# Moving single steps of a written-out order: chunk attention with an FFN on one core

## The chip, the core and the metric

The kernel runs on one core of a Trainium2 chip. A core has engines that run side by side, each with an instruction line of its own that it works off in order: TensorE for matmuls (PE; its loading of weights is PEld), VectorE (DVE), ScalarE (ACT), GpSimd (POOL) and SyncE (SP), which here issues all the DMAs. The metric is the device time of one execution in microseconds (us); smaller is better.

## The reference

Attention in chunks of 64 rows, and on its output, laid side by side for the 8 heads, a feed-forward layer, all in fp32:

```python
batch, n_heads, seq, head_dim = (8, 8, 576, 64)          # chunk = 64
scores = scale * np.matmul(q_c, k_c.transpose(0, 1, 2, 4, 3))   # per chunk: 64 x 64
scores = scores - np.max(scores, axis=-1, keepdims=True)
attn = np.exp(scores)
attn = attn / (np.sum(attn, axis=-1, keepdims=True) + 1e-09)
out = np.matmul(attn, v_c)
x = np.ascontiguousarray(attn_out.transpose(0, 2, 1, 3)).reshape(B * S, H * D)   # 4608 x 512
h = x @ w_in                                              # 512 x 2048
g = h * (1.0 / (1.0 + np.exp(-1.702 * h)))
return (g @ w_out).astype(np.float32)                     # 2048 x 512
```

## The kernel before

**The work.** Every large product is done in fp32 precision with three matmuls, since each operand is split in a high and a low part (x_h, x_l; g_h, g_l): low times high, high times high, high times low. The 4608 rows of x are 36 tiles of 128. Attention runs over pairs of tiles, named by the first tile u of the pair (tq0_16 is a step of the pair 16, 17). For one pair, function plan_pair loads q and k into one buffer "raw" (lines 953, 964), turns them with two big transposes on DVE, tq0 and tq1 (1007), makes scores s on PE (1023), their maximum mx and the difference m on DVE (1031, 1040), exp on ACT (1043), the sum z on DVE (1047 to 1050), the normalisation on POOL (1053), transposes et on DVE (1072), and x on PE (1097). "raw" comes free when tq1 has read it, and only then may the next pair's loads start.

**The FFN** runs over 9 blocks of 512 rows (4 tiles) and 16 slices of 128 columns of w_in; g numbers slices through all blocks, so that 0 to 15 are block 0 and 32 is the first of block 2. For a slice: h0_g and h_g on PE (1245), gelu and its high part gh_g on ACT, the low part gl_g on DVE (1272), then o_g_0 to o_g_3 on PE (1282 to 1284), one for each tile, which add to four sums po0 to po3. After a block's last slice a sum is copied out by ob_n_t (n the block, t the tile): by ACT for t even (1291), by DVE for t odd (1293), into one of two buffers "ob"; the store st_n_t (1298) is issued on SP, and its landing frees the buffer. The sum of the next block can't start before the copy is done.

**Blocks 0 and 1** are computed so. Block 2 (plan_seven) and the pairs of blocks 3 to 8 (plan_two, numbered 0 to 2 by r) get x @ w_in from seven products of half-size pieces instead of eight. In block 2 the products' matmuls are ph0_g to ph3_g (715 to 717), their drains on DVE d0_g to d3_g (719), the low part of gelu gl_g (756). The pieces of w_in are sums and differences made on DVE (612, steps plo and pout with their high parts on ACT) and POOL (592 to 601), stored to DRAM (628) and loaded again (702, ld0_g to ld3_g; 801). The pieces of x come from subtractions (535, steps t1 to t4 with x_r_h behind; plan_x), whose engine the table ON_POOL sets: POOL for r = 0, DVE for the rest.

**The order** is written out before the program is built. The class Plan takes every step with an engine, a cost in us, a rank, the events that it needs and makes, and the buffers that it takes and gives; `emit` plays it through and, whenever an engine is free, gives it the ready step of the lowest rank. A DMA's landing is reckoned from constants (ISSUE, LANDING, LANES). The engines' lines are then fixed in the order so found, and at run time each engine waits at the head of its line, whatever stands behind. The first steps up to about 60 us come from a list of names, ORDER.

Of the kernel before, what the change touches and what calls it, by code (L numbers as in the profile page):

```python
# [47 lines left out]
class Plan:  # L48
# [7 lines left out]

    ISSUE, LANES, LANDING = 0.48, 8, 2.1
    TABLE_LOAD = 1.3

    def __init__(self, buffers):  # L60
        self.free = dict(buffers)
        self.steps = []
        self.landed = [0.0] * self.LANES
        self.first = {}


    def add(self, engine, cost, rank, fn, need=(), make=None, take=(), give=(), table=None, port=False):
        self.steps.append((engine, cost, rank, fn, tuple(need), make, tuple(take), tuple(give), table, port or engine == POOL))
# [4 lines left out]
    def transfers(self, now, count, each):  # L73

        for _ in range(count):
            start = max(now, self.landed[-self.LANES])
            now = start + self.ISSUE
            self.landed.append(max(start + self.LANDING, self.landed[-1] + each))
        return now, self.landed[-1]

    def emit(self):
        waits, users, ready = {}, {}, {e: [] for e in self.HANDOVER}
        at = []
# [16 lines left out]
        while left:  # L100
            for e, heap in ready.items():
                while heap and busy[e] <= now + 1e-9:
# [11 lines left out]
                    if pick is None:  # L114
                        break
                    _, cost, _, fn, _, make, take, give, tab, port = self.steps[pick]
                    if first.get(e):
# [15 lines left out]
                    busy[e] = now + cost  # L133
                    post(done, 0, give)
                    if e != DMA:
# [26 lines left out]
def tile_chunk_attention_ffn(  # L162
# [14 lines left out]
    P = 128  # L177
# [4 lines left out]
    TB = 4  # L182
# [66 lines left out]
    def plan_w(j):  # L249
# [98 lines left out]
    def plan_first(u):  # L348
# [171 lines left out]
    def plan_x(r, h, ua, uc, rank):  # L520
# [266 lines left out]
    def plan_two(s, p):  # L787
# [137 lines left out]
    def plan_pair(u):  # L925
# [198 lines left out]
        if pe:  # L1124
            for t in range(2):
                plan.add(
                    DMA, (2, 0.85), rank - 3, lambda t=t: load_qk_rows(t), need=[ev("rows0")] if t else [],
                    make=ev(f"rows{t}"), take=[] if t else [raw_tag],
# [13 lines left out]
        else:  # L1142
# [83 lines left out]
    def plan_ffn(g):  # L1226
# [104 lines left out]
        for t in range(TB):  # L1331
# [83 lines left out]
```

## Time and profile before

| | |
|---|---|
| median of 3 runs | 845.12 us (843.11 to 847.92) |
| the profiled execution | 844.18 us |
| its span, first to last instruction | 842.4 us, so 1.8 us lie around it |
| mean granted TensorE clock | 0.993 of full |
| busy: PE, PEld, DVE, ACT, POOL | 818.4, 680.0, 549.1, 378.4, 86.7 us |
| DMA | 128.96 MB, mean 153 GB/s |

The rows in the prediction are read so. A row of busy time by stretch gives the stretch and its length, then for PE, PEld, DVE, ACT and POOL the busy time and (x) the number of instructions, then the granted clock of TensorE, the busy share of the DMA engines and the GB/s. A row of waits says who waited for whom: total, times, longest. A row of a timeline has the start, the duration, the engine and the line of the kernel, the operation and its operands (out<-in, buffer numbers left out), the shape, and in brackets how long the engine had been idle before it and what ended that. SPq is SP's line of DMA issues: their duration is that of the issuing, not of the transfer. 512-wide matmuls start 0.23 us apart when nothing holds them, though each is shown with 0.39.

### The profile page before, as it was taken

What the parts mean: (1) busy time and instruction counts of PE and PEld (TensorE: products, weight loads), DVE (VectorE), ACT (ScalarE), POOL (GpSimd) and SP (SyncE); (2) the same over time, 40 slices, a digit from 0 to 9 for tenths busy, and PEclk for the clock granted to TensorE, in tenths of its full rate; (3) what the DMA queues carried; (4) which work ended last, traced back from release to release, by engine and by line L of the source; (5) the groups of instructions that cost most, each with busy time, mean ns of one, the idle gap of its engine ahead of it and who ended that gap; (6) DMA issues with size and microseconds to landing.
All of it is one profiled execution on the core that took longest, in us unless ns stands there. A gap on an engine that the chain in (4) does not pass through costs nothing.

```text
span 842.4 us, 15212 instructions
## 1 busy us (share of the span) xinstructions
PE 818.4 (97%) x5894; PEld 680.0 (81%) x5894; DVE 549.1 (65%) x781; ACT 378.4 (45%) x557; POOL 86.7 (10%) x78
## 2 busy tenths in 40 slices
PE   7999998999979999999999999999999999999998
PEld 6878886877878888778888888888888888888786
DVE  5769967566867888874776995393778453443422
ACT  5989825345344436342534433342555323223322
POOL 1000163563200000000000100000001000000000
PEclk9999999999989999999999999999999999999999
DMA  9997856775488776575466336466541054444101
GB/s 227 313 309 239 251 130 163 208 202 134 129 244 218 212 209 141 169 175 147 125 179 176 62 79 173 126 152 155 145 128 49 1 165 121 118 122 126 50 1 51
DMA packets 238248, 128.96 MB, mean 153 GB/s; under 512 B 186464, under 2 KB 208992, under 8 KB 238176
## 3 DMA queue, kind: packets, MB, share of 16 engines
q1 hardware_dynamic: 238176, 127.98, 56.5%
q8 instruction: 47, 0.77, 0.4%
q14 instruction: 25, 0.20, 0.1%
HBM read 103.81 MB, written 24.12 MB: 152 GB/s over the span
## 4 chain that ended last, share of the span: by engine, by line
PE 81%; SPq 9%; DMA 4%; DVE 3%; issue 1%; ACT 1%; POOL 0%; DVEq 0%; ACTq 0%; POOLq 0%
PE po L1282 14%; PE po L1283 13%; PE po L1284 13%; PE hp L810 9%; PE hp L811 9%; PE hp L812 9%; SPq L964 3%; SPq L338 2%; PE hp L1245 2%; PE hp L1246 2%; PE hp L1247 2%; DMA w<-seven 2%; PE s L1023 2%; PE x L1097 1%; SPq L258 1%
## 5 line engine op out<-in xcount | busy, mean ns | idle before, releaser
L1282 PE MATMUL po<-w,g_l 128*128 128x512 f32 x576 | 228.1, 396 | 6.7 <-ACT ob L1291 4.8
L1283 PE MATMUL po<-w,g_h 128*128 128x512 f32 x576 | 225.0, 391 | 0.0
L1284 PE MATMUL po<-w,g_h 128*128 128x512 f32 x576 | 224.8, 390 | 0.0
L1282 PEld LDWEIGHTS po<-w,g_l 128*128 128x128 f32 x576 | 108.5, 188 | 32.3 <-ACT ob L1291 5.5
L1284 PEld LDWEIGHTS po<-w,g_h 128*128 128x128 f32 x576 | 108.4, 188 | 23.0
L1283 PEld LDWEIGHTS po<-w,g_h 128*128 128x128 f32 x576 | 108.5, 188 | 21.1
L848 ACT ACTIVATE g<-g 128x512 f32<-128x512 f32 x48 | 30.3, 632 | 143.3 <-DVE g L795 143.1
L1072 DVE STREAM_TRANSPOSE eT<-e 32x512 f32<-32x512 f32 x120 | 84.2, 701 | 5.4 <-POOL e L1053 3.5
L810 PE MATMUL hp<-w,w 128*128 128x512 f32 x224 | 87.4, 390 | 0.2
L811 PE MATMUL hp<-w,w 128*128 128x512 f32 x224 | 87.2, 389 | 0.0
L812 PE MATMUL hp<-w,w 128*128 128x512 f32 x224 | 87.2, 389 | 0.0
L1053 POOL TENSOR_TENSOR e<-e,r 128x1024 f32<-128x1024 f32 x16 | 32.2, 2012 | 502.1 <-DVE r L1050 397.6
L857 DVE TENSOR_TENSOR g_l<-g,g_h 128x512 fp32r<-128x512 f32 x48 | 35.2, 737 | 44.5 <-ACT g_h L853 44.2
L853 ACT ACTIVATE g_h<-g 128x512 fp32r<-128x512 f32 x48 | 30.3, 631 | 73.7 <-PE po L1284 71.4
L1007 DVE STREAM_TRANSPOSE qkT<-raw 128x1024 f32<-128x1024 f32 x30 | 37.2, 1241 | 27.8 <-DMA raw<-in_k_dram 15.7
L1245 PE MATMUL hp<-x_l,w 128*128 128x512 f32 x120 | 47.8, 398 | 5.8 <-DVE g_l L1272 5.8
L810 PEld LDWEIGHTS hp<-w,w 128*128 128x128 f32 x224 | 42.0, 188 | 9.9 <-DVE f L795 0.5
L812 PEld LDWEIGHTS hp<-w,w 128*128 128x128 f32 x224 | 42.0, 188 | 8.8
L811 PEld LDWEIGHTS hp<-w,w 128*128 128x128 f32 x224 | 42.0, 188 | 8.6
L1247 PE MATMUL hp<-x_h,w 128*128 128x512 f32 x120 | 47.4, 395 | 0.0
L1246 PE MATMUL hp<-x_h,w 128*128 128x512 f32 x120 | 47.4, 395 | 0.0
L795 DVE TENSOR_TENSOR d<-hp,d 128x512 f32<-128x512 f32 x48 | 32.9, 684 | 19.0 <-PE hp L812 18.7
(142 smaller groups left out, 1335.5 us busy)
## 6 DMA issues: line engine op xcount, KB each, us to landing
w<-seven SPq DMA_DIRECT2D x120, 256.0 KB, 2.9
pieces<-seven SPq DMA_DIRECT2D x56, 256.0 KB, 2.9
seven<-w SPq DMA_DIRECT2D x24, 512.0 KB, 3.7
w<-seven SPq DMA_DIRECT2D x24, 512.0 KB, 4.6
raw<-in_moe_w_in_dram SPq DMA_DIRECT2D x16, 512.0 KB, 7.5
raw<-in_moe_w_out_dram SPq DMA_DIRECT2D x16, 512.0 KB, 7.8
out_dram<-ob SPq DMA_DIRECT2D x32, 256.0 KB, 2.3
raw<-in_q_dram SPq DMA_DIRECT2D x208, 32.0 KB, 2.4
```

The source lines that it names most:

```text
L810: nc.tensor.matmul(hp, w[:, 0, c], xl[:, c], start=c == 0, stop=False)
L811: nc.tensor.matmul(hp, w[:, 0, c], xh[:, c], start=False, stop=False)
L812: nc.tensor.matmul(hp, w[:, 1, c], xh[:, c], start=False, stop=c == 1)
L857: nc.vector.tensor_tensor(gl, words(h, late), gh.bitcast(F32), op=ALU.subtract)
L1007: nc.vector.transpose(st["tr"][:, i].rearrange("p n (t j) -> p (n t) j", j=32), st["raw"][:, i].rearrange("p n t j -> p (n t) j"),)
L1072: nc.vector.transpose(st["et"][po : po + 32, :, 32 * a : 32 * a + 32], st["e"][pi : pi + 32, :, 32 * b : 32 * b + 32],)
L1245: nc.tensor.matmul(hp, wh, xl, start=cc == 0, stop=False)
L1246: nc.tensor.matmul(hp, wh, xh, start=False, stop=False)
L1247: nc.tensor.matmul(hp, wl, xh, start=False, stop=cc == NCC - 1)
L1282: nc.tensor.matmul(po, gl[:, c], w[:, 0, :], start=first, stop=False)
L1283: nc.tensor.matmul(po, gh[:, c], w[:, 0, :], start=False, stop=False)
L1284: nc.tensor.matmul(po, gh[:, c], w[:, 1, :], start=False, stop=last)
```

## The change

The constants and ranks of the planner change, and a table NUDGE adds an offset to the rank of 38 single steps. The model of a DMA gets a limit on pieces in flight (PIECES); LANDING goes from 2.1 to 1.8; the 16 pairs get other RANKS; stores get a rank 40 ahead of their slice instead of 22 (STORE); the high and low parts of late slices get 7.5 instead of 1.5 (GLATE); the pieces of weights are made a step nearer or further (LEAD, SUMS); and POOL does the subtractions of r = 2 as well (ON_POOL), eight instructions. Nothing else is computed otherwise: all other instructions are the same, with the same shapes, on the same engines. ORDER isn't changed.

```diff
-    ISSUE, LANES, LANDING = 0.48, 8, 2.1
+    ISSUE, LANES, LANDING = 0.48, 8, 1.8
+    PIECES = 3072
...
+        rank += self.nudge.get(make, 0.0)
...
             start = max(now, self.landed[-self.LANES])
+            while True:
+                flight = [(t, n) for t, n in self.flight if t > start]
+                if sum(n for _, n in flight) + pieces <= self.PIECES:
+                    break
+                start = flight[0][0]
             now = start + self.ISSUE
-            self.landed.append(max(start + self.LANDING, self.landed[-1] + each))
+            self.landed.append(max(start + self.LANDING, self.landed[-1]) + each)
...
-    RANKS = (-10.5, 9.0, 14.0, 21.0, 26.5, 28.5, 35.0, 39.0, 45.5, 49.5, 61.0, 72.0, 76.5, 85.5, 94.0, 101.5)
+    RANKS = (-14.0, 8.5, 15.5, 21.0, 26.5, 30.5, 34.5, 39.5, 45.5, 54.5, 59.5, 76.5, 77.0, 78.5, 94.0, 101.5)
...
-    LEAD = 27
+    LEAD = 28
...
-    SUMS = 3
-    ON_POOL = (0,)
+    SUMS = 2
+    GLATE = 7.5
+    XLATE = 0.5
+    STORE = 40
...
+    NUDGE = {
+        "ph0_36": -2.0, "o_15_1": 2.0, "ph2_40": -12.5, "o_12_2": 6.5, "o_63_1": -1.5, "o_36_3": 1, "d0_0_3":
...
+    ON_POOL = (0, 2)
...
-            at = o_rank(g) - 1.5 if late else rank - 5
+            at = o_rank(g) - GLATE if late else rank - 5
...
-                    DMA, (len(list(spans((n * TB + t) * P, P))), 0.72), rank - 22, lambda t=t: o_store(t), need=[f"ob_{n}_{t}"],
+                    DMA, (len(list(spans((n * TB + t) * P, P))), 0.72), rank - STORE, lambda t=t: o_store(t), need=[f"ob_{n}_{t}"],
```

Lines of the kernel after the change are 25 to 27 further down (1298 is 1324, 1007 is 1033, 1272 is 1298, 756 is 782). What the change does to the lines of the engines is shown at three places. A row has the line, the operation, out<-in with the buffers' full names, the shape, and a count where alike instructions follow one another.

DVE in the second half of block 0, before and after. g_l_14 is the output of gl_14, the two transposes of raw_8 are tq0_8 and tq1_8, the copies ob_0_1 and ob_0_3 drain block 0:

```order
L1007 STREAM_TRANSPOSE qkT_8_1303<-raw_8_1069 128x1024
L1272 TENSOR_TENSOR g_l_14_1295<-hp_14_1226,g_h_14_1294 128x512
L1007 STREAM_TRANSPOSE qkT_8_1303<-raw_8_1069 128x1024
L1272 TENSOR_TENSOR g_l_15_1348<-hp_15_1287,g_h_15_1347 128x512
L1031 TENSOR_REDUCE m_8_1437<-s_8_1361 128x16
```

```order
L314 TENSOR_TENSOR w_15_1220<-wtmp_15_1164,w_15_1220 128x2x512
L1033 STREAM_TRANSPOSE qkT_8_1291<-raw_8_1067 128x1024 x2
L1298 TENSOR_TENSOR g_l_14_1305<-hp_14_1232,g_h_14_1304 128x512
L1298 TENSOR_TENSOR g_l_15_1337<-hp_15_1296,g_h_15_1336 128x512
L1057 TENSOR_REDUCE m_8_1438<-s_8_1358 128x16
```

Both transposes now stand ahead of gl_14. A little later in the same line z_8 goes behind gl_17 and two of the weight sums of line 612.

SP at the end of block 1, before and after. raw_16 is loaded in four lots of eight and more, w_7 and so on are weights' pieces, out_0_dram<-ob_1_t is st_1_t:

```order
L702 DMA w_7_754<-seven_80 128x1024
L953 DMA raw_16_2182<-in_k_dram 32x4x32 x8
L702 DMA w_8_821<-seven_80 128x512
L702 DMA w_0_331<-seven_80 128x1024
L953 DMA raw_16_2182<-in_k_dram 32x4x32 x8
L1298 DMA out_0_dram<-ob_1_0_2461 128x512
L1298 DMA out_0_dram<-ob_1_1_2474 128x512
L338 DMA v_14_2573<-in_v_dram 128x8x64
L702 DMA w_1_446<-seven_80 128x1024
L953 DMA raw_16_2182<-in_k_dram 32x4x32 x8
L702 DMA w_5_650<-seven_80 128x1024
```

```order
L728 DMA w_7_754<-seven_80 128x1024
L979 DMA raw_16_2180<-in_k_dram 32x4x32 x8
L1324 DMA out_0_dram<-ob_1_0_2441 128x512
L728 DMA w_8_821<-seven_80 128x512
L1324 DMA out_0_dram<-ob_1_1_2511 128x512
L979 DMA raw_16_2180<-in_k_dram 32x4x32 x8
L1324 DMA out_0_dram<-ob_1_2_2551 128x512
L728 DMA w_0_328<-seven_80 128x1024
L728 DMA w_1_440<-seven_80 128x1024
L979 DMA raw_16_2180<-in_k_dram 32x4x32 x8
L1324 DMA out_0_dram<-ob_1_3_2596 128x512
L728 DMA w_5_644<-seven_80 128x1024
```

The first two stores go ahead of a lot of eight loads, the third ahead of the last lot, and the weights w_0 and w_1 go behind.

DVE at the same place, before and after. g_l_32 is gl_32, d_32 and f_32 are what the drains d0 to d3 write, w_10 and w_12 are steps l0x and l1x on pieces of x, raw_16 is read by tq0_16 and tq1_16:

```order
L1293 COPY ob_1_1_2474<-po_1_1_1548 128x512
L756 TENSOR_TENSOR g_l_32_2477<-d_32_2395,g_h_32_2476 128x512
L1007 STREAM_TRANSPOSE qkT_16_2551<-raw_16_2182 128x1024
L1031 TENSOR_REDUCE m_14_2562<-s_14_2480 128x16
L719 TENSOR_TENSOR f_32_2453<-hp_32_3_2564,d_32_2395 128x256
L1040 TENSOR_TENSOR e_14_2561<-s_14_2480,m_14_2562 128x1024
L1293 COPY ob_1_3_2608<-po_1_3_1560 128x512
L756 TENSOR_TENSOR g_l_33_2605<-f_32_2453,g_h_33_2604 128x512
```

```order
L1319 COPY ob_1_3_2596<-po_1_3_1562 128x512
L576 TENSOR_TENSOR w_10_963<-xs_12_2529,w_9_881 128x2x256
L782 TENSOR_TENSOR g_l_32_2585<-d_32_2395,g_h_32_2584 128x512
L576 TENSOR_TENSOR w_12_1023<-xs_12_2529,w_11_1017 128x2x256
L782 TENSOR_TENSOR g_l_33_2600<-f_32_2563,g_h_33_2599 128x512
L745 TENSOR_TENSOR d_34_2618<-hp_34_0_2570,d_34_2618 128x256
L745 TENSOR_TENSOR d_34_2618<-hp_34_1_2603,d_34_2618 128x256 x2
L1073 TENSOR_REDUCE z_14_2642<-e_14_2535 128x16
L1074 TENSOR_SCALAR z_14_2642<-z_14_2642 128x16
L1076 RECIPROCAL r_14_2645<-z_14_2642 128x16
L1033 STREAM_TRANSPOSE qkT_16_2519<-raw_16_2180 128x1024
L745 TENSOR_TENSOR d_34_2618<-hp_34_2_2647,d_34_2618 128x256
```

gl_32 stood right behind ob_1_1 and stands now behind ob_1_3; tq1_16 stands ahead of the last drains of slice 34 (d2_34, d3_34), which it followed before. On ACT ob_1_2 goes ahead of gh_32, with the first two high parts of x's pieces behind it, and on PE o_32_0 and o_32_1 go behind ph1_34.

More of the change, by code (lines that the diff above doesn't have):

```diff
@@ L63, in __init__, with add, transfers @@
         self.landed = [0.0] * self.LANES
+        self.flight = []
         self.first = {}
-    def add(self, engine, cost, rank, fn, need=(), make=None, take=(), give=(), table=None, port=False):
-        self.steps.append((engine, cost, rank, fn, tuple(need), make, tuple(take), tuple(give), table, port or engine == POOL))
+        self.nudge = {}
+    def add(self, engine, cost, rank, fn, need=(), make=None, take=(), give=(), table=None, port=False, after=0.0):
+        rank += self.nudge.get(make, 0.0)
+        self.steps.append((engine, cost, rank, fn, tuple(need), make, tuple(take), tuple(give), table, port or (engine == POOL and not after), after))
     def bulk(self, cost, rank, fn, need=(), make=None, take=(), give=()):
         self.add(DMA, (1, cost), rank, fn, need=need, make=make, take=take, give=give)
-    def transfers(self, now, count, each):
+    def transfers(self, now, count, each, pieces=256):
         for _ in range(count):
             start = max(now, self.landed[-self.LANES])
+            while True:
[3 more added lines that the diff above has]
+                start = flight[0][0]
             now = start + self.ISSUE
-            self.landed.append(max(start + self.LANDING, self.landed[-1] + each))
+            self.landed.append(max(start + self.LANDING, self.landed[-1]) + each)
+            self.flight = flight + [(self.landed[-1], pieces)]
         return now, self.landed[-1]
@@ L115, in emit @@
                         break
-                    _, cost, _, fn, _, make, take, give, tab, port = self.steps[pick]
+                    _, cost, _, fn, _, make, take, give, tab, port, after = self.steps[pick]
                     if first.get(e):
@@ L133, in emit @@
                     busy[e] = now + cost
-                    post(done, 0, give)
+                    post(done + after, 0, give)
                     if e != DMA:
@@ L191, in tile_chunk_attention_ffn @@
     NH = 2
-    RANKS = (-10.5, 9.0, 14.0, 21.0, 26.5, 28.5, 35.0, 39.0, 45.5, 49.5, 61.0, 72.0, 76.5, 85.5, 94.0, 101.5)
+    RANKS = (-14.0, 8.5, 15.5, 21.0, 26.5, 30.5, 34.5, 39.5, 45.5, 54.5, 59.5, 76.5, 77.0, 78.5, 94.0, 101.5)
     K_ACT = (1, 2, 3, 4)
-    LEAD = 27
+    LEAD = 28
     PREP = -3
-    SUMS = 3
-    ON_POOL = (0,)
+    SUMS = 2
+    GLATE = 7.5
+    XLATE = 0.5
+    STORE = 40
+    OBODD = 0.0
+    RLATE = 0
+    NUDGE = {
[6 rows of a table added]
+    }
+    ON_POOL = (0, 2)
     RING_2 = (7, 8, 0, 1, 5, 6)
@@ L297, in plan_w @@
         e = lambda n: f"{n}_{j}"
-        plan.add(DMA, (2, 1.56), rank - 5.5, load, need=need, make=e("raw"), take=[f"w{j}"])
+        plan.add(DMA, (2, 1.5, 384), rank - 5.5, load, need=need, make=e("raw"), take=[f"w{j}"])
         plan.add(ACT, 1.08, rank, scale, need=[e("raw")], make=e("wsc"))
@@ L457, in plan_first @@
         rank = u - 95
-        plan.add(DMA, (1, 1.2), u - 103, lambda: load(0), make=ev("q"), take=[slot(0)])
-        plan.add(DMA, (1, 1.2), u - 102.9, lambda: load(1), make=ev("k"))
-        plan.add(DMA, (1, 0.9), u - 101.5, load_v, make=ev("v"), take=[slot(1)])
+        plan.add(DMA, (1, 1.2, 1024), u - 103, lambda: load(0), make=ev("q"), take=[slot(0)])
+        plan.add(DMA, (1, 1.2, 1024), u - 102.9, lambda: load(1), make=ev("k"))
+        plan.add(DMA, (1, 0.9, 1024), u - 101.5, load_v, make=ev("v"), take=[slot(1)])
         plan.add(PE, 0.45, rank, lambda: t_pe(0), need=[ev("q")], make=ev("tqp"), take=["hp"])
@@ L551, in lo @@
             nc.vector.tensor_tensor(conv(i, k, 1), form(raw(i, k)), conv(i, k, 0).bitcast(F32), op=ALU.subtract)
+        rank += XLATE
         e = lambda a: f"{a}x_{r}_{h}"
@@ L1126, in plan_pair @@
                 plan.add(
-                    DMA, (2, 0.85), rank - 3, lambda t=t: load_qk_rows(t), need=[ev("rows0")] if t else [],
+                    DMA, (2, 0.85, 1024), rank - 3, lambda t=t: load_qk_rows(t), need=[ev("rows0")] if t else [],
                     make=ev(f"rows{t}"), take=[] if t else [raw_tag],
@@ L1148, in plan_pair @@
                     plan.add(
-                        DMA, (count, 0.18), rank - ahead, lambda i=i, n=n: load_qk(i, n),
+                        DMA, (count, 0.18), rank - ahead - RLATE, lambda i=i, n=n: load_qk(i, n),
                         need=raw[:1] if i + n else [f"qk_1_{NP - 1}_{u - 2}"] if u - 2 >= NPE else [], make=ev(f"qk_{i}_{n}"),
@@ L1159, in plan_pair @@
             plan.add(
-                DMA, (2, 0.85) if pe else (len(list(spans(u * P, P))), 0.9), rank - (7 if pe else 1.5), lambda t=t: load_v(t), need=[ev("v0")] if t else [], make=ev(f"v{t}"),
+                DMA, (2, 0.85, 512) if pe else (len(list(spans(u * P, P))), 0.9, 1024), rank - (7 if pe else 1.5), lambda t=t: load_v(t), need=[ev("v0")] if t else [], make=ev(f"v{t}"),
                 take=[] if t else ["v"],
@@ L1341, in plan_ffn @@
                 plan.add(
-                    eng, 0.6, rank - 3.5, lambda t=t: o_out(t), need=[f"o_{g}_{t}"],
+                    eng, 0.6, rank - 3.5 + OBODD * (t % 2), lambda t=t: o_out(t), need=[f"o_{g}_{t}"],
                     make=f"ob_{n}_{t}", take=[tag], give=[f"po{t}"],
@@ L1367, in tile_chunk_attention_ffn @@
         plan.first[e] = names
+    plan.nudge.update(NUDGE)
     for u in range(TB):
```

5 rows, old and new, of the table NUDGE are left out of this document.

## The prediction

> **What bounds the kernel now.** I read the page first, then busy time by stretch, then the waits of TensorE (PE), then the timelines of the four other queues round its longest waits.
>
> ```profile
> span 842.4 us, 15212 instructions
> PE 818.4 (97%) x5894; PEld 680.0 (81%) x5894; DVE 549.1 (65%) x781; ACT 378.4 (45%) x557; POOL 86.7 (10%) x78
> ```
>
> PE is busy 97% of the span, so only 842.4 - 818.4 = 24.0 us are idle, plus what a lowered clock costs. The columns of the next view are PE, PEld, DVE, ACT, POOL busy, the granted PE clock, the DMA share, GB/s.
>
> ```profile
> 126.00:147.00 21.00, 17.66 (x72) 14.08 (x71) 14.59 (x20) 10.53 (x15) 7.32 (x7) 0.92 0.64 164
> 147.00:210.00 63.00, 60.55 (x502) 49.52 (x501) 38.48 (x47) 28.80 (x43) 29.63 (x30) 1.00 0.67 183
> 210.00:253.00 43.00, 38.17 (x326) 33.73 (x325) 32.45 (x49) 17.89 (x28) 7.45 (x6) 0.92 0.65 185
> 253.00:320.00 67.00, 65.23 (x742) 57.63 (x742) 56.06 (x95) 28.77 (x45) 3.81 (x2) 1.00 0.77 204
> 320.00:400.00 80.00, 79.46 (x470) 65.03 (x469) 59.05 (x88) 33.83 (x51) 3.81 (x2) 1.00 0.64 162
> 400.00:800.00 400.00, 399.60 (x2524) 329.08 (x2523) 243.32 (x351) 155.13 (x241) 11.94 (x6) 1.00 0.45 119
> ```
>
> From 400 to 800 PE idles 0.40 us: nothing can be won there, only lost. What can be won lies from 126 to 400: idle 3.34, 2.45, 4.83, 1.77 and 0.54. Two stretches also run at 0.92 of the clock, which costs 0.08 x 21 = 1.7 and 0.08 x 43 = 3.4. The whole prize is 12.9 + 5.1 = 18.0, or 2.1%. The start and the tail, the rest of the idle time, keep their order.
>
> ```profile
> PE hp L1245 <- DVE g_l L1272: 5.8, 3, 3.3
> PE po L1282 <- ACT ob L1291: 4.8, 1, 4.8
> ```
>
> Two waits hold 3.3 and 4.8 of it. Their releasers are copies that had waited themselves, so I follow each back.
>
> **Block 0's stores.** PE, SP and DVE, first the matmul h0_18:
>
> ```profile
> 129.72 0.39 PE L1247 MATMUL hp<-x_h,w 128*128 128x512 f32 x1
> 133.45 0.50 PE L1245 MATMUL hp<-x_l,w 128*128 128x512 f32 x1 [3.34 <-DVE g_l L1272]
> 134.92 0.63 PE L1247 MATMUL hp<-x_h,w 128*128 128x512 f32 x1
> 128.67 0.87 SPq L1298 DMA_DIRECT2D out_dram<-ob  x2
> 130.97 0.69 DVE L1293 COPY ob<-po 128x512 f32<-128x512 f32 x1 [6.15 <-DMA out_dram<-ob]
> 132.72 0.68 DVE L1272 TENSOR_TENSOR g_l<-hp,g_h 128x512 fp32r<-128x512 f32 x1
> 116.81 0.39 PE L1282 MATMUL po<-w,g_l 128*128 128x512 f32 x1
> 117.52 1.25 DVE L1007 STREAM_TRANSPOSE qkT<-raw 128x1024 f32<-128x1024 f32 x1 [3.31 <-DMA raw<-in_k_dram]
> ```
>
> The drain at 130.97 waited for the landing of a store that SP issued at 128.67, and g_l stood behind it in DVE's line. After the wait matmuls take 0.63 instead of 0.39. In the new order these stores keep their place on SP (st_0_3 alone goes behind a v load, 0.45), so the release at 133.45 stays. But tq1_8, the transpose of 117.52, now stands ahead of gl_14. It ends at 118.77, gl_14 at about 119.4, and o_14_0, which ran at 116.81, waits 2.6 for it. That wait comes out of the 3.34: the idle time is split in 2.6 and 0.7 and costs nothing new. What it may end is the lowered clock. The 1.56 below was followed by 0.39 to 0.40; 3.34 by 0.63.
>
> ```profile
> 202.45 0.50 PE L1245 MATMUL hp<-x_l,w 128*128 128x512 f32 x1 [1.56 <-DVE g_l L1272]
> 202.79 0.40 PE L1246 MATMUL hp<-x_h,w 128*128 128x512 f32 x1
> ```
>
> 2.6 lies between them. I take no lowered clock: **-1.7** (0 to -1.7).
>
> **Block 1's stores.** SP, DVE, ACT, PE:
>
> ```profile
> 232.03 0.86 SPq L702 DMA_DIRECT2D w<-seven  x2
> 236.78 0.85 SPq L1298 DMA_DIRECT2D out_dram<-ob  x2
> 238.91 4.31 SPq L953 DMA_DIRECT2D raw<-in_k_dram  x8
> 238.99 0.69 DVE L1293 COPY ob<-po 128x512 f32<-128x512 f32 x1 [4.86 <-DMA out_dram<-ob]
> 239.59 0.68 DVE L756 TENSOR_TENSOR g_l<-f,g_h 128x512 fp32r<-128x512 f32 x1
> 240.28 0.60 ACT L1291 ACTIVATE ob<-po 128x512 f32<-128x512 f32 x1 [5.95 <-DMA out_dram<-ob]
> 235.70 0.28 PE L716 MATMUL hp<-w,w 128*128 128x256 f32 x1
> 235.82 0.28 PE L717 MATMUL hp<-w,w 128*128 128x256 f32 x1
> 240.93 0.79 PE L1282 MATMUL po<-w,g_l 128*128 128x512 f32 x1 [4.83 <-ACT ob L1291]
> ```
>
> Here o_32_2 waits for ob_1_2, which waits for a store issued at 236.78, behind weights and 8 raw loads. In the new order st_1_0 goes where the weights went at 232.03 and st_1_1 one load later (+0.9): with the same time from issue to landing (236.78 to 238.99, 2.2; the second, issued at 237.2, to 240.28, 3.0) they land near 234.2 and 236.0. The gain isn't 4.7, because other steps moved too. ob_1_3 and one l0x (0.69 each) now stand ahead of gl_32 on DVE: 236.0 + 0.69 + 0.69 + 0.68 = 238.1. And o_32_0 and o_32_1 (6 matmuls, 1.4) moved behind ph1_34, so when PE goes on at 238.1 instead of 240.9 it has 1.4 more to do: **-1.5** (0 to -4.8). Its wait is then 238.1 - 234.7 = 3.4 (234.7 is the 236.1 at which PE ran dry, less those 1.4), near the 3.34 that lowered the clock. Of the 3.4 of lost clock I take about half, **-1.5** (0 to -3.4).
>
> The Trainium skill, TensorE: Matmul & The Clock Gate, section "What's actually happening", says that the array falls to half clock after an idle window of about 3.4 us and that the window runs freely, so that a wait of this length may or may not fill one. The rows 1.56, 3.34 and 4.83 agree; by it this term is either 0 or -3.4.
>
> **tq1_16** now stands ahead of d2_34 and d3_34 on DVE. Its last loads were issued until 243.2 and, in the new order, at nearly the same time (two stores and w_0, w_1 ahead of them, v_14 behind). With the 2.2 to land and 1.25 for the transpose, DVE is free at about 246.5. PE goes on at 238.1, has seven o steps (0.68 each) and ph2_34 and ph3_34 (18 matmuls, 0.12 from start to start in the rows 235.70 and 235.82) to do, 7.0 in all, and at 245.1 it wants for ph0_36 the buffer that d2_34 drains: a wait of about 1.7, or none if its own clock is low, or 3.0 if the store gain is larger. **+1.5** (0 to +3.0).
>
> **Raw loads of pair 12.** z_8 (the sum of pair 8's exponentials) moved behind gl_17 and two L612 steps (weight sums).
>
> ```profile
> 135.32 1.18 DVE L1047 TENSOR_REDUCE z<-e 128x16 f32<-128x1024 f32 x1
> 136.91 0.63 DVE L1272 TENSOR_TENSOR g_l<-hp,g_h 128x512 fp32r<-128x512 f32 x1
> 147.80 0.68 DVE L612 TENSOR_TENSOR w<-sums,w 128x512 fp32r<-128x512 f32 x1
> 148.40 1.24 DVE L1007 STREAM_TRANSPOSE qkT<-raw 128x1024 f32<-128x1024 f32 x1
> 149.67 4.59 SPq L964 DMA_DIRECT2D raw<-in_q_dram  x8
> ```
>
> So z_8 starts 0.63 + 2 x 0.68 = 2.0 later; the normalisation on POOL, eight transposes of e and tq1_10 (148.40) follow it in line, and the loads that wait for tq1_10's buffer start 2.0 later than 149.67, or 3.3 with another L1072 pair ahead. Everything that SP has to issue behind them slips. Whether a later stretch takes this up no row shows: 0 to +3.3, and I take **+2.0**, since PE already waits 2.45 in 147 to 210.
>
> **The other single steps**, some thirty swaps that change no count, can each put a short wait on PE, as here:
>
> ```profile
> 182.02 0.50 PE L1245 MATMUL hp<-x_l,w 128*128 128x512 f32 x1 [0.89 <-DVE g_l L1272]
> ```
>
> I take one such, **+1.0** (0 to +2.5), and of the idle 1.77 + 0.54 in 253 to 400 half goes, **-1.2** (0 to -2.3).
>
> **Eight subtractions** of block pair 2 (L535) go from DVE to POOL.
>
> ```profile
> L535 DVE TENSOR_TENSOR xt<-xs x8: 670/686/693, 455.9 to 652.4; 128x512 f32<-128x512 f32 x8
> L535 POOL TENSOR_TENSOR xt<-xs x2: 1296/1299/1302, 203.7 to 206.4; 128x512 f32<-128x512 f32 x2
> 137.14 1.90 POOL L1053 TENSOR_TENSOR e<-e,r 128x1024 f32<-128x1024 f32 x1 [17.61 <-DVE r L1050]
> 137.45 2.13 DVE L612 TENSOR_TENSOR w<-sums,w 128x512 fp32r<-128x512 f32 x1
> ```
>
> POOL gains 8 x 1.30 = 10.4, DVE loses 8 x 0.69 = 5.5. The four of a chain end 4 x 0.61 = 2.4 later. DVE is 61% busy there, so its time off the path is the cover: **0** (-0.4 to +4.9). The upper end is what the last two rows price: L612, 0.68 alone, took 2.13 and ended 0.5 behind POOL's; if every POOL step held DVE for its whole length, DVE would stand 10.4 and save 5.5.
>
> The Trainium skill, SBUF — State Buffer, "SBUF: two separate sides", says that the two engines share a port pair under an exclusive lock, and the waiting one is blocked for the whole instruction. The rows agree, and it speaks against this move; by it the term would be +4.9, less whatever DVE's slack covers.
>
> **The sum.** -1.7 - 1.5 - 1.5 + 1.5 + 2.0 + 1.0 - 1.2 + 0 = -1.4. The profiled execution took 844.18 (0.94 below the median of 845.12), so it would take 842.8 and the median **843.7**. A difference under 0.5%, 4.2 us, can't be told from none here.
>
> **Rivals.**
> - *Both store waits go with their clock*: -1.7, -4.8 + 1.4, -3.4, -1.2, +1.0 = -8.7, **836.4**. For it: 3.34 + 4.83 + 5.1 = 13.3 of the 18.0 hang on the stores of these two blocks, and block 1's land earlier. Against: DVE's line ahead of gl_32. It decides whether gl_32 is done by 236, which asks a landing of st_1_1 2 us sooner than I worked out.
> - *Slower: a transpose that waits for a load holds DVE.* tq1_16 stands ahead of the drains; st_1_2, which waits for ob_1_2, stands ahead of its last loads on SP. If ob_1_2 comes after 237.4, when SP gets there, the loads slip, and PE's wait for d2_34 passes the 3.3 that lowers the clock: -1.7 - 1.5 + 0 + (3.0 + 1.7) + 3.3 + 2.5 - 1.2 = +6.1, **851**. For it: the 6.15 and 5.95 waits above are of this kind. Against: 2.5 of margin by the landing of st_1_0.
> - *POOL holds DVE*: -1.4 + 4.9 = +3.5, **848.6**. For it the 2.13; against it 39% idle DVE and 0.40 idle PE in that stretch.
> - *Nothing happens*: waits move along the chain and end at the same landings; 845, inside the forecast's case.
>
> **How the numbers follow.** Forecast's case, 839.5 to 848: 0.48 (0.08 faster, 0.38 same, 0.02 slower). Store waits gone: 0.28 (0.25 faster, 0.03 same). DVE held by a load: 0.16 (0.14 slower, 0.02 same). POOL: 0.08 (0.05 same, 0.03 slower). That gives 0.33, 0.48, 0.19. The range 836 to 850 leaves out about 0.1 below, in the first rival, and 0.1 above, in the second.
>
> **What would show it.** A wait of about 2.6 before o_14_0 at 117, under 1 before h0_18, and 1.00 in 126 to 147; SP's L1298 stores near 232 to 233, and PE's wait before o_32_0 of 3 to 3.5 ending near 238; a wait for DVE near 245; pair 12's first load near 152; POOL's L535 at 12 of them, with DVE two-input steps beside them at over 1 us. I'm wrong if h0_18's release moves away from 133.45, if the wait at block 1 is under 1 or its clock is full, or if PE idles over 2 us anywhere in 400 to 800.

## The result, and the profile after

| | median of 20 runs | ratio to before, 95% interval |
|---|---|---|
| before | 845.22 us | |
| after | 849.25 us (846.16 to 852.39) | 1.0048 (1.0032 to 1.0064) |
| after, measured again later beside the experiments | 846.88 us, before 844.95 | 1.0038 (1.0018 to 1.0058) |

The change makes the kernel some 3 to 4 us slower. The forecast was 843.7, 1.4 below before: the measured time lies inside the range given, but the sign is wrong. The profiled execution of after took 850.78, more than its median, and that of before 844.18, less than its median; so part of what differs between these two traces is chance. A second profiled execution of after took 846.99 (label e_again) and is set beside the first below.

First the page and the same stretches as before (PE, PEld, DVE, ACT, POOL busy, PE clock, DMA share, GB/s):

```profile
span 848.6 us, 15206 instructions
PE 818.6 (96%) x5894; PEld 679.1 (80%) x5894; DVE 549.8 (65%) x773; ACT 376.1 (44%) x555; POOL 99.5 (12%) x86
...
126.00:147.00 21.00, 21.00 (x94) 17.35 (x93) 12.88 (x20) 11.60 (x18) 8.21 (x9) 1.00 0.71 190
147.00:210.00 63.00, 56.57 (x477) 46.07 (x477) 37.45 (x48) 26.94 (x40) 26.82 (x28) 0.97 0.60 164
210.00:253.00 43.00, 39.51 (x329) 33.84 (x328) 31.33 (x49) 18.52 (x30) 9.26 (x7) 0.96 0.64 176
253.00:320.00 67.00, 61.91 (x612) 54.59 (x610) 54.50 (x93) 27.57 (x43) 3.81 (x2) 1.00 0.81 215
320.00:400.00 80.00, 79.33 (x594) 65.75 (x594) 61.37 (x90) 35.08 (x52) 3.81 (x2) 1.00 0.62 156
400.00:800.00 400.00, 398.02 (x2518) 328.02 (x2518) 244.02 (x343) 152.04 (x238) 23.93 (x14) 1.00 0.45 118
```

PE works as long as before (818.6 against 818.4 us) and idles 30.0 us instead of 24.0. The first row is the success of the change: from 126 to 147 PE is busy throughout at full clock, where it idled 3.34 and ran at 0.92. The next rows say where that went. In 147 to 210 the idle time is 6.43 instead of 2.45, and the clock is lowered there, which it wasn't before (0.97 instead of 1.00). In 253 to 320 the idle time is 5.09 instead of 1.77, in 400 to 800 1.98 instead of 0.40. Only 210 to 253 is better: 3.49 instead of 4.83, with the clock at 0.96 instead of 0.92.

The waits behind these numbers, in PE's timeline:

```profile
119.72 0.50 PE L1308 MATMUL po<-w,g_l 128*128 128x512 f32 x1 [1.39 <-DVE g_l L1298]
204.24 0.80 PE L1271 MATMUL hp<-x_l,w 128*128 128x512 f32 x1 [4.67 <-DVE g_l L1298]
241.62 0.71 PE L1308 MATMUL po<-w,g_l 128*128 128x512 f32 x1 [2.84 <-DVE g_l L782]
273.67 0.39 PE L741 MATMUL hp<-w,w 128*128 128x256 f32 x1 [2.00 <-DVE d L745]
282.80 0.50 PE L1308 MATMUL po<-w,g_l 128*128 128x512 f32 x1 [1.86 <-DVE g_l L782]
431.45 0.50 PE L1308 MATMUL po<-w,g_l 128*128 128x512 f32 x1 [1.34 <-DVE g_l L883]
```

The same places in the second profiled execution of after:

```profile
147.00:210.00 63.00, 58.96 (x486) 47.65 (x485) 39.04 (x49) 28.44 (x42) 28.68 (x29) 0.97 0.63 171
202.15 0.50 PE L1271 MATMUL hp<-x_l,w 128*128 128x512 f32 x1 [3.29 <-DVE g_l L1298]
238.77 0.50 PE L1308 MATMUL po<-w,g_l 128*128 128x512 f32 x1 [2.02 <-DVE g_l L782]
248.20 0.38 PE L741 MATMUL hp<-xe,w 128*128 128x256 f32 x1 [2.19 <-DVE d L745]
```

The wait at 204 is the largest of the first trace, and it is new in size, not in place: in before, PE waited 1.56 there, and was released at 202.45. It is 4.67 in one execution of after and 3.29 in the other. Behind it the clock is lowered in both, which costs 1.7 more. Followed back on DVE, SP and POOL in the first trace:

```profile
202.36 1.25 DVE L1033 STREAM_TRANSPOSE qkT<-raw 128x1024 f32<-128x1024 f32 x1 [8.43 <-DMA raw<-in_k_dram]
203.53 0.65 DVE L1298 TENSOR_TENSOR g_l<-hp,g_h 128x512 fp32r<-128x512 f32 x1
152.27 1.81 SPq L990 DMA_DIRECT2D raw<-in_q_dram  x4
139.97 1.29 POOL L618 TENSOR_TENSOR whole<-w 128x512 f32<-128x512 f32 x1
141.22 1.91 POOL L1079 TENSOR_TENSOR e<-e,r 128x1024 f32<-128x1024 f32 x1
137.86 1.22 DVE L1073 TENSOR_REDUCE z<-e 128x16 f32<-128x1024 f32 x1 [1.07 <-ACT e L1069]
```

DVE stands 8.43 us at tq1_14 for the last load of pair 14, with g_l behind it. Those loads come behind those of pair 12, which began at 152.27 instead of 149.67, 2.60 later. Two moved steps lie ahead of them. One is z_8, the sum of pair 8's exponentials on DVE: it starts at 137.86, in before at 135.32, 2.54 later, behind gl_17 and two weight sums and then 1.07 more behind the exponential. The other is n_8, the normalisation of pair 8 on POOL, which needs z_8's result. It now stands behind four sums and a copy and runs at 141.22, some 1.6 after that result is there; in before it ran at 137.14, as the first of them. The transposes of e, then tq1_10, which frees the buffer raw, wait for it. From the start of z_8 to the first load it takes 14.41 here (15.07 in the second trace) and 14.35 in before, so in this order the lateness of z_8 is most of the delay.

At 430 the same pattern stands in a row of its own: tq1_26 waits for its load, and gl_59, which stood ahead of it before, waits behind.

```profile
429.57 1.25 DVE L1033 STREAM_TRANSPOSE qkT<-raw 128x1024 f32<-128x1024 f32 x1 [2.51 <-DMA raw<-in_k_dram]
430.74 0.65 DVE L883 TENSOR_TENSOR g_l<-f,g_h 128x512 fp32r<-128x512 f32 x1
```

### The profile page after: what moved, and what is told of

It reads as the page before. It is cut to its first block, busy times and chain, and to the rows that moved or that the text cites. A ratio compares the mean times of both kernels' runs of the same rounds, so it can differ in the third digit from the quotient of the medians.

```text
span 848.6 us, 15206 instructions
## 1 busy us (share of the span) xinstructions
PE 818.6 (96%) x5894; PEld 679.1 (80%) x5894; DVE 549.8 (65%) x773; ACT 376.1 (44%) x555; POOL 99.5 (12%) x86
## 4 chain that ended last, share of the span: by engine, by line
PE 68%; SPq 12%; DMA 8%; DVE 6%; issue 3%; ACT 2%; DVEq 0%; ACTq 0%
PE po L1308 12%; PE po L1309 12%; PE po L1310 12%; PE hp L836 9%; PE hp L837 9%; PE hp L838 9%; SPq L990 6%; DMA v<-in_v_dram 3%; SPq L363 2%; SPq L283 1%; PE x L1123 1%; PE s L1049 1%; DMA seven<-w 1%; DMA raw<-in_k_dram 1%; SPq L287 1%
```

## The experiments

The theory of the loads: up to about 300 us the releases that PE waits for are the landings at the end of SP's line of loads. A gain that PE makes ahead of such a place is lost there; a delay of the line stays. The rival is the prediction's sum: every part keeps what it wins. A second rival puts the loss after 250 us.

For all of these but the repeat, the list of steps that the planner found (for before or for after) is written into the changed kernel and single steps are moved in it, so nothing else moves with them. Line numbers are some 165 to 190 higher for it. Each ratio is to the kernel before, run beside it on the same chip. Two traces are compared by the time at which PE starts the same matmul in both, since executions are up to 2 or 3 us apart already at 100 us.

**One step of the change put into before: tq1_8 (e_tq8).**

```diff
 DVE of before
-tq0_8 gl_14 tq1_8 gl_15
+tq0_8 tq1_8 gl_14 gl_15
```

> The kernel before with one step moved: tq1_8 ahead of gl_14 on DVE, as the change has it. Theory of the loads: PE waits about 1.5 to 2.6 before o_14_0 at 117, the wait of 3.3 before h0_18 and the lowered clock after it go, PE is 1.7 to 2.2 ahead at 145, and loses it again at 200, where the wait for g_l behind the last loads of pair 14 grows from 1.6 to 3.3 to 3.8: time as before, 845. Rival, the terms add: the 1.7 to 2.2 stay to the end, 843 to 843.5.

Measured: 843.38, ratio 0.9980 (0.9963 to 0.9998). PE idled 2.80 before o_14_0 and not at all from 126 to 147, near what the prediction had said (2.6 and 0.7). By the time the rival came out, and the wait at 200 did not grow (0.91). But this trace doesn't show a gain at the place: the lowered clock only moved with the wait (0.97 in 60 to 126, 1.00 in 126 to 147), and PE is 1.9 ahead of the trace of before at 150, of which 1.3 were there before 100. So it doesn't test whether a gain is lost at 200. Moving one step ahead of one g_l isn't what lost.

**n_8 back in after (e_n8).**

```diff
 POOL of after
-psum_2 pa0_3 n_8 pa_3
+n_8 psum_2 pa0_3 pa_3
```

> The changed kernel with one step moved back: n_8, the normalisation of pair 8 on POOL, ahead of psum_2 and the copies of the weights' sums. Theory of the loads: pair 12's first load starts at 149.7 to 151 instead of 152.3, each later release of the same loads comes 1 to 2 earlier, the wait at 199 falls from 4.7 to 3 to 3.7, and the time is 1 to 2 below the changed kernel's, 847 to 848.3. Rival, the loss is made after 250 us: 849, and any gain at 200 is lost at the next wait.

Measured: 846.62, 1.0025 (1.0009 to 1.0041). Pair 12's first load, on SP, and z_8, on DVE:

```profile
150.22 1.81 SPq L1155 DMA_DIRECT2D raw<-in_q_dram  x4
136.29 1.22 DVE L1238 TENSOR_REDUCE z<-e 128x16 f32<-128x1024 f32 x1 [0.74 <-ACT e L1234]
```

The load is 2.05 earlier than in the first trace of after, but z_8, which doesn't depend on this move, is already 1.57 earlier: 0.5 is left for n_8, and 1.1 beside the second trace. The wait at 200 was 3.87, between the 3.29 and the 4.67 of the two traces of after; from 140 to 208 PE gains 2.0 on the first of them and nothing on the second. The time is near what the theory gave (847 to 848.3), not the rival's 849, but the interval overlaps those of after (1.0048 and 1.0038). So a cost of n_8 in the order of after isn't shown by this run.

**tq1_26 back in after (e_tq26).**

```diff
 DVE of after
-tq1_26 gl_59 d1_0_6 d2_0_6 gl_60 d3_0_6
+gl_59 d1_0_6 d2_0_6 gl_60 d3_0_6 tq1_26
```

> The changed kernel with one step moved back: tq1_26 behind gl_59, d1, d2, gl_60 and d3 of slice pair 6 on DVE, where it stood before. Theory of a transpose that holds DVE: the wait of 1.3 before o_59_0 at 430 goes and nothing takes its place, 847.5 to 848. Rival, the wait only moves on (the buffer raw comes free 1 to 4 later, and so do the loads behind it): 849.

Measured: 846.54, 1.0018 (1.0002 to 1.0034); the wait before o_59_0 is gone and none came in its place (PE busy 399.24 in 400 to 800). From 400 us to the end PE needs 1.5 less than in the second trace of after, about the 1.34 of the wait. The time is below the theory's 847.5 to 848; its interval just overlaps that of after.

**Before up to 267 us, then after (e_split).**

```diff
 all engines
-the list of after
+the list of before up to o_36_0, then the rest in the list of after
```

> The order of before up to o_36_0 (at 267 us), the order of the change from there, its eight subtractions on POOL among it. Theory of the loads, the loss is made before 280: 844 to 846.5, with the one wait of about 1.3 before o_59_0. Rival, the loss is made in the second part (subtractions on POOL, later loads of pair 18 and on): 848.5 to 851.

Measured: 845.74, 1.0016 (0.9999 to 1.0032). The second part of the change costs about 1.3 by this (0 to 2.7), and the wait at o_59_0 (1.18 in this trace) is as much. By the medians the larger part of the loss is made ahead of 267, but the intervals of this ratio and of those of after overlap.

**Block 1's first two stores earlier, in before (e_st1).**

```diff
 SP of before
-qk_1_1_16 ld3_34 ld0_36 qk_1_2_16 st_1_0 st_1_1
+qk_1_1_16 st_1_0 ld3_34 st_1_1 ld0_36 qk_1_2_16
```

> The kernel before with one thing moved: the stores st_1_0 and st_1_1 go ahead of two weights' loads and eight raw loads on SP, nothing else. Theory of the loads (PE is released by the last loads of a pair, so a gain made just ahead of such a place is lost there): the wait of 4.8 before o_32_2 falls under 1 and the clock stays at 1.00, PE is 4 to 7 ahead at 243, and waits so much more before o_34 to o_36 (up to 267), where gl_36 stands behind tq0_18 and its loads: 842.5 to 845. Rival, the terms add: minus 4.8 and minus 2.9 for the clock stay, 837 to 839.

Measured: 844.85, 1.0015 (0.9996 to 1.0034). This is the clearest answer to the prediction's way of adding. Three rows of PE:

```profile
235.46 0.50 PE L1473 MATMUL po<-w,g_l 128*128 128x512 f32 x1 [1.50 <-ACT ob L1482]
247.97 0.56 PE L1473 MATMUL po<-w,g_l 128*128 128x512 f32 x1 [3.07 <-DVE g_l L947]
268.25 0.50 PE L1473 MATMUL po<-w,g_l 128*128 128x512 f32 x1 [4.22 <-DVE g_l L947]
```

The wait of 4.83 fell to 1.50 (under 1 was expected), and waits of 3.07 before a g_l and of 4.22 at o_36 came behind it. At the first, before has no wait; at the second it has 0.40 in its trace and 1.52 in that of e_poolb, whose order is the same there. DVE stood 3.58 at tq1_16 and 5.21 at tq0_18 for loads, with the g_l behind them, and both waits were followed by a lowered clock. PE was 2.1 ahead of before at 208, 8.2 at 250 and 2.1 behind at 275. The stores' landing was the longest wait in the trace of before, and shortening it by 3.3 gains nothing.

**n_8 and tq1_26 both back (e_both).**

```diff
 POOL and DVE of after
+both moves of e_n8 and e_tq26
```

> The changed kernel with two steps back at their old places, n_8 ahead of psum_2 on POOL and tq1_26 behind d3 of slice pair 6 on DVE. If the two losses add, 1.9 and 2.5 as the single moves measured: 4.4 below the changed kernel's time, 844.5 to 845.5, the same as before. If they overlap: 846 to 847.

Measured: 844.83, 1.0019 (1.0002 to 1.0035). By the median it is the time forecast, by the ratio it's no better than either move alone. The intervals are too wide to say whether the two losses add: inconclusive by itself.

**The subtractions on DVE in after (e_nopool), and on POOL in before (e_poolb).**

```diff
-    ON_POOL = (0, 2)
+    ON_POOL = (0,)
```

> The changed kernel, every step at its place, with the eight subtractions of block pair 2 on DVE again, as before. Forecast's value, the move costs nothing: 849 (847.5 to 850.5). Rival, POOL holds DVE by the shared port: the waits of 0.2 and 0.5 near 467 and 511 go, and up to 4.9 come back: 844 to 847.

> The kernel before, every step at its place, with the eight subtractions of block pair 2 on POOL instead of DVE, and nothing else. By the traces so far (0.6 idle at 467 and 511 that goes with them): 0.5 to 1.5 above before. My forecast's value: 0. Rival, the shared port for the whole length: up to 4.9 above.

Measured: 845.43 (beside a before of 843.74), 1.0024 (1.0010 to 1.0039) without them in after; 844.88, 1.0010 (0.9989 to 1.0031) with them in before. The rows of after in the stretches that have them, and of e_nopool:

```profile
440.00:470.00 30.00, 29.82 (x250) 24.40 (x249) 21.07 (x27) 15.38 (x27) 5.84 (x4) 1.00 0.63 161
490.00:520.00 30.00, 29.54 (x248) 23.92 (x247) 19.36 (x22) 12.39 (x19) 6.15 (x4) 1.00 0.25 64
```

```profile
440.00:470.00 30.00, 30.00 (x252) 24.85 (x251) 20.67 (x32) 15.61 (x27) 0.00 (x0) 1.00 0.63 159
490.00:520.00 30.00, 30.00 (x252) 24.88 (x251) 19.86 (x30) 12.54 (x20) 0.00 (x0) 1.00 0.30 78
```

POOL's column shows the eight steps, PE's column 0.18 + 0.46 = 0.64 idle that goes with them. On DVE in after, beside them:

```profile
463.97 1.78 DVE L576 TENSOR_TENSOR w<-xt,w 128x512 fp32r<-128x512 f32 x1
465.67 1.77 DVE L883 TENSOR_TENSOR g_l<-g,g_h 128x512 fp32r<-128x512 f32 x1
```

Steps that take 0.68 alone take 1.77, as the Trainium skill, SBUF — State Buffer, "SBUF: two separate sides", has it: held for the whole of POOL's step. PE has other work there, so most of it doesn't reach the end. But more reaches it than the 0.64 of idle time. Across these steps (from 455 to 530 us) PE needs 1.4 more in after than in e_nopool, at the same matmuls; the same 1.4 to 1.5 stands between e_both and e_fix3 and between e_best and e_best3 (both further down), pairs that also differ in these steps, and 0.7 between e_poolb and before. A wait is shown some 0.16 too short, since a matmul is shown with 0.39 though the next can start after 0.23; this is a part of the difference.

The times of four pairs of kernels point the same way: 1.0048 and 1.0038 to 1.0024 for e_nopool, 1.0019 to 0.9985, 1.0010 to 0.9984, and 1.0010 to 1 for e_poolb, which is 0.8 to 2.9 us. The intervals of each pair overlap. The 845.43 of e_nopool lies in the range of its rival (844 to 847), below that of "costs nothing". The rival's full +4.9 is excluded for the order of before (at most 0.3% more, 2.6 us).

**All three undone (e_fix3).**

```diff
 after
+n_8 ahead of psum_2 on POOL, tq1_26 behind d3_0_6 on DVE, ON_POOL = (0,)
```

> The changed kernel with three steps undone: n_8 ahead of psum_2 on POOL, tq1_26 behind d3 of slice pair 6 on DVE, the eight subtractions on DVE. If these three are the loss, it takes what before takes, within 1 us, and TensorE's waits over 1 us at 430 and those of 0.2 to 0.5 near 467 and 511 are gone. If the loss lies in the many other moves: 2 or more above before, though these waits are gone.

> The changed kernel itself, unaltered, beside the others of this call on one chip: what it loses to the kernel before here. As first measured: 848 to 849.5 where before takes 844.5.

Measured on the same chip: e_fix3 844.03, 0.9985 (0.9964 to 1.0006); after itself (e_again) 846.88, 1.0038 (1.0018 to 1.0058). Undoing three steps of the many takes back the whole loss: the intervals don't meet. (By "three steps" the eight subtractions count as one.) In the trace of e_fix3, its slowest execution (847.53), the waits after 400 are gone, as expected; those before are not: 3.05 at 203, 2.62 at 249, 1.78 at 273 and 1.86 at 282. So the traces show what two of the three steps give back, 1.5 for tq1_26 and 1.4 for the subtractions; what n_8 gives they don't show.

**The same two steps put into before (e_n8b, e_tq26b).**

```diff
 POOL of before (e_n8b)
-n_8 psum_2 pa0_3 pa_3
+psum_2 pa0_3 n_8 pa_3
 DVE of before (e_tq26b)
-gl_59 d1_0_6 et_24 d2_0_6 gl_60 d3_0_6 tq1_26
+tq1_26 gl_59 d1_0_6 et_24 d2_0_6 gl_60 d3_0_6
```

> The kernel before with one step moved: n_8 on POOL behind psum_2 and pa0_3 (four sums and a copy), as the change has it. Theory (the loads of pair 12 and all behind them come later): their first load at 151 to 153 instead of 149.7, the waits at 180 and 200 (0.9 and 1.6) longer by 1.5 to 2.5 together, 0.8 to 2.2 above before at the end. Rival, the later loads are caught up before PE needs them: as before, within 0.5.

> The kernel before with one step moved: tq1_26 on DVE ahead of gl_59, d1, d2, gl_60 and d3 of slice pair 6, as the change has it. Theory (DVE stands for a load with PE's next operand behind it): a wait of 1 to 2 before o_59_0 at 424 that isn't made up, 1 to 2 above before. Rival, the load has landed by then in the order of before: as before, within 0.5.

Measured: e_n8b 850.74, 1.0056 (1.0031 to 1.0082); e_tq26b 849.42, 1.0049 (1.0021 to 1.0076). Either step alone costs before 4 to 5 us, more than I expected. The rows, of e_n8b POOL, SP and PE, then of e_tq26b DVE and PE and the stretch they lie in:

```profile
141.86 1.90 POOL L1243 TENSOR_TENSOR e<-e,r 128x1024 f32<-128x1024 f32 x1
153.37 3.83 SPq L1154 DMA_DIRECT2D raw<-in_q_dram  x8
145.99 0.50 PE L1435 MATMUL hp<-x_l,w 128*128 128x512 f32 x1 [2.77 <-DVE g_l L1462]
184.01 0.50 PE L1435 MATMUL hp<-x_l,w 128*128 128x512 f32 x1 [2.62 <-DVE g_l L1462]
204.89 0.50 PE L1435 MATMUL hp<-x_l,w 128*128 128x512 f32 x1 [2.00 <-DVE g_l L1462]
```

```profile
428.56 1.25 DVE L1198 STREAM_TRANSPOSE qkT<-raw 128x1024 f32<-128x1024 f32 x1 [3.22 <-DMA raw<-in_k_dram]
431.04 0.50 PE L1001 MATMUL hp<-w,w 128*128 128x512 f32 x1 [3.19 <-DVE d L986]
400.00:440.00 40.00, 36.81 (x273) 29.55 (x273) 23.66 (x34) 13.66 (x20) 1.91 (x1) 0.96 0.56 145
```

In the first, n_8 runs 4.7 later than in before, pair 12's loads begin 3.7 later, and PE waits at 146 (no such wait in before), 184 (0.89 in before) and 205 (1.56), the last followed by a lowered clock. From z_8 to the first load it now takes 19.3 instead of 14.35. PE, which was 3.0 ahead of before at 140, is 4.0 behind at 208 and 6.0 at the end. In the second, DVE stands 3.22 for a load and PE 3.19 behind it, and the clock is lowered for another 1.7 (0.96 of 40 us); that is more than the 1 to 2 expected. Neither is made up later.

**A version that beats both (e_best2), and tq1_8 on top (e_best3).**

```diff
 all engines
+the list of before up to o_36_0, then that of after with tq1_26 behind d3_0_6, ON_POOL = (0,)
+(e_best3) and tq1_8 ahead of gl_14
```

> The order of before up to o_36_0 and that of the change from there, with tq1_26 at its old place and the eight subtractions on DVE. If the second part of the change holds a gain of about 1 that these two steps hid: 1 to 2 below before. If not: as before, within 0.7.

> The version that was the fastest so far (the order of before up to o_36_0, then the change's, tq1_26 at its old place, subtractions on DVE) with tq1_8 ahead of gl_14. If moving tq1_8 is worth the 1.6 that it measured alone: 840 to 841.5, 1.2 to 2 below that version beside a kernel before of 845. If the gain is lost at the loads of pair 14: 842 to 843, as that version.

An earlier mixture (e_best), the same as e_best3 with the subtractions on POOL:

> The order of before up to o_36_0 and that of the change from there, with tq1_8 ahead of gl_14 and tq1_26 at its old place behind d3 of slice pair 6. If the parts add as measured, 1.0 for the split, minus 1.7 for tq1_8, minus 2.5 for tq1_26: 3 below the kernel before, 841 to 842.5. If they don't: 843.5 to 845.

It was no faster than before: 844.74, 1.0010 (0.9991 to 1.0028), so the parts did not add.

Measured: e_best2 841.96, 0.9968 (0.9946 to 0.9990), below both kernels. Its stretches, against 0.54 and 0.40 idle in before:

```profile
320.00:400.00 80.00, 80.00 (x478) 66.29 (x477) 60.04 (x89) 34.41 (x52) 3.81 (x2) 1.00 0.64 163
400.00:800.00 400.00, 399.91 (x2530) 330.51 (x2529) 242.04 (x351) 153.20 (x240) 11.94 (x6) 1.00 0.44 118
```

So the second part of the change holds a small gain that two steps hid, tq1_26 and the subtractions: in the traces PE needs 1.5 less from 420 us to the end than in before. e_best3 took 843.50, 0.9984 (0.9959 to 1.0009): tq1_8 adds nothing to it, against what it did alone, and the time lies above both expectations.

## Why the prediction was wrong, point by point

The gains came about as forecast; the losses were mis-sized. Counted in idle time and lowered clock beside the trace of before, the first trace of after gains 3.0 from 60 to 147 and 3.0 in 210 to 253; it loses 5.7 in 147 to 210, 3.5 in 253 to 400 and 1.6 in 400 to 800. For the second trace the gains are 1.8 and 3.5, the losses 3.3, 2.3 and 1.5. What was to show the forecast mostly appeared (the wait before o_14_0, the full clock from 126 to 147, the start near 152), and no sign of being wrong looked at 204, where most was lost.

**What bounds the kernel** was read half. The two store waits were the longest, and I took them for the prize. I did not ask what PE runs into next. Before's own trace had it: in 147 to 210 PE waits 1.56 at 202 for a g_l behind a transpose for which DVE had stood 5.32 on a load. It also waits 0.89 at 182, at the end of a chain (a sum z, POOL, the transposes of e) that starts at a transpose for which DVE had stood 3.23. The transpose of the first, in before:

```profile
200.58 1.25 DVE L1007 STREAM_TRANSPOSE qkT<-raw 128x1024 f32<-128x1024 f32 x1 [5.32 <-DMA raw<-in_k_dram]
```

e_st1 shows the price of that omission: 6.1 won from 208 to 250, and 10.3 lost again by 275.

**Block 0's stores, -1.7.** The mechanism was right in the change: a wait moved ahead (2.6 forecast, 1.39 and 2.67 in the two traces of after), none before h0_18, the clock full. That the clock stays full behind the moved wait was luck: behind 2.80 at this place in e_tq8, and 2.30 in e_best, it was lowered. Put alone into before, the step measured -1.7 (-0.2 to -3.1), and +1.4 on top of e_best2, within the intervals of both. In the change the gain is gone at 204, where PE waits 4.67 (3.29) for a landing that no work of PE brings forward; that it is lost there for this reason fits e_st1, but no run takes this one gain apart.

**Pair 12's loads, +2.0, start near 152.** This is the step that failed. The start was right: 152.27, and so in the main was the cause, z_8, 2.54 later where 2.0 was forecast. n_8 on POOL, whose line I did not read at that place, comes on top, with 0.5 to 1.1 of the start in this order. What was wrong is the price. I took 2.0 with a bound of 3.3, by the time that the loads slip. Measured in 147 to 210: 4.0 and 1.6 more idle time, and 1.7 of lowered clock behind the wait at 204, in both traces of after. That makes 5.7 and 3.3, and the clock had no term here at all. PE was 2.2 ahead of before at 140 in both, and was released at 204.24 and 202.15 instead of 202.45: that gain brought the release forward by 0.3 at most.

**Block 1's stores, -1.5 and -1.5.** The wait was forecast as 3.4 ending at 238.1. In the first trace it is 2.84 and ends at 241.62, since SP gets to st_1_0 at 234.90 instead of 232.0; in the second, st_1_0 is issued at 232.60 and the wait is 2.02 and ends at 238.77. The clock of the stretch came to 0.96, half of the loss back, in the first, and to 1.00 in the second. This was right, and better than forecast.

**tq1_16, +1.5.** PE's wait here was 0.19 in the first trace of after and 2.19 in the second, within the 0 to 3.0 given. With single steps moved ahead of it or behind, the same place gave up to 3.83 (e_nopool), so the bound was too low.

**The other single steps, +1.0 in all, and -1.2 for the small waits.** One of them, tq1_26, costs 1.5 in after by the traces, and 4.1 (1.8 to 6.4) when put into before. I had looked for moved transposes at pairs 8 and 16, not through the rest of DVE's line. And the small waits from 253 to 400 did not shrink: 5.76 idle and 4.62 in the second trace, instead of 2.31. (In other traces with before's order here it is 4.06, e_poolb, and 4.67, e_tq26b, so 2.31 was luck.) Of these, 2.00 stand behind tq0_18, and 1.86, the same in all seven traces of this order, before an o step whose g_l stands behind six transposes of e on DVE.

**The subtractions, 0.** They cost 1.4 in the order of after by three pairs of traces that differ in them, of which 0.64 shows as idle time, and an effect between -0.9 and +2.6 us in before's order. The cover that I named, DVE's slack, held for most of the 4.9, not for all.

**The rival that came true** in kind is the second: a transpose that waits for a load holds DVE. I gave it 0.16, at tq1_16, on the ground of 2.5 us of margin; DVE stood 2.65 and 2.78 there. It also happened at tq1_14, tq0_18 and tq1_26, which the rival did not name. What n_8 and tq1_26 cost depends on the order round them. n_8 late delays the first load by 5.0 in before, counted from z_8, and by 0.5 to 1.1 in after; behind tq1_26, PE waits 3.19 and the clock is lowered in e_tq26b, 1.34 and the clock is full in after. What stays open is how much n_8 costs in after: the run gives 1 to 2 us with intervals that overlap, the traces less than they differ among themselves.

## What to carry to other kernels

A wait is worth removing only if what PE needs next is already there: before pricing it, look for the following release that comes from a transfer, and cap the gain there. When an order is changed, follow each in-order queue past each moved step, the idlest engine included: here a normalisation behind five short steps on an engine that is busy 10% of the time cost 4.7 us (2.6 to 6.9). Give every wait that grows a term for the lowered clock behind it. A step that waits for a transfer should not stand ahead of what the bounding engine reads next. And before a shift between two traces is put down to a moved step, look how far apart they are ahead of that step: of 2.05 us here, 1.57 were.

## What the runs showed of the hardware that was not expected

Whether a wait lowers TensorE's clock isn't set by its length alone. The same wait of 1.86 us at the same step was followed by matmuls of 0.63 in e_fix3 and of 0.40 in e_both; one of 2.90 in e_best was followed by 0.40:

```profile
281.77 0.67 PE L1473 MATMUL po<-w,g_l 128*128 128x512 f32 x1 [1.86 <-DVE g_l L947]
282.24 0.63 PE L1474 MATMUL po<-w,g_h 128*128 128x512 f32 x1
279.91 0.50 PE L1473 MATMUL po<-w,g_l 128*128 128x512 f32 x1 [1.86 <-DVE g_l L947]
280.25 0.40 PE L1474 MATMUL po<-w,g_h 128*128 128x512 f32 x1
269.80 0.50 PE L1473 MATMUL po<-w,g_l 128*128 128x512 f32 x1 [2.90 <-DVE g_l L947]
270.14 0.40 PE L1474 MATMUL po<-w,g_h 128*128 128x512 f32 x1
```

The granted clock in the traces of this case shows what decides. Every lowered stretch between 60 and 800 us lasts 3.41 or 6.83 us, at half clock, and costs 1.7 or 3.4. Within one trace their starts lie whole multiples of 3.413 us apart (31 of them in before, 34 and then 6 in e_st1), so each execution has a fixed grid of such stretches. Where PE idled over 2.06 us of one stretch, the clock was lowered in the next, in all 29 cases of the 17 traces. Where it idled 0.9 to 1.72, it never was, in 58 cases. Between 1.73 and 2.04 it was in 8 of 17. (Stretches that are lowered themselves are left out.) The wait of 1.86 lies inside one stretch in e_fix3 (1.80 idle), and across two in e_both (1.12 and 0.74); the 2.90 of e_best are split in 1.43 and 1.47. Two stretches of e_fix3, then the two of e_best and the next, with the clock in the third column from the end:

```profile
278.29:281.71 3.42, 1.62 (x14) 1.42 (x12) 3.35 (x6) 0.38 (x1) 0.00 (x0) 1.00 0.85 230
281.71:285.12 3.41, 3.35 (x10) 2.78 (x11) 3.20 (x7) 0.00 (x0) 0.00 (x0) 0.53 0.58 166
```

```profile
264.92:268.33 3.41, 1.98 (x17) 1.77 (x15) 0.40 (x1) 3.35 (x6) 0.00 (x0) 1.00 0.69 126
268.33:271.74 3.41, 1.94 (x8) 1.61 (x9) 3.31 (x6) 1.82 (x2) 0.00 (x0) 1.00 0.97 265
271.74:275.15 3.41, 3.41 (x25) 3.19 (x24) 3.31 (x9) 0.29 (x1) 1.11 (x1) 1.00 1.12 254
```

The Trainium skill, TensorE: Matmul & The Clock Gate, "What's actually happening", names an idle window of about 3.4 us, which runs freely. The length and the free run agree with these traces; a whole window of idle time was not needed here, some 2 us of it were enough, and the measurement decides. Where the grid falls is luck of each execution, so a wait of about 2 to 3 us may cost 1.7 more or nothing.
